# Second layer of a fused attention and feed-forward kernel: products and units of a step in longer runs

## The chip, the cores and the metric
The kernel runs on one NeuronCore of a Trainium2 chip. The metric is the device time of one execution in microseconds. Three executions of the kernel before took 962.70, 963.16 and 963.23 us; the median is 963.16 us. Two such times that lie within 0.2% of each other cannot be told apart.

## The reference
Attention with an exponential feature map, then two feed-forward layers over 2304 tokens, with model width 512 and inner width 2048. The change touches the last line alone.

```python
x = attn_out.transpose(0, 2, 1, 3).reshape(B * S, H * D)      # 2304 x 512
h = x @ w_in                                                  # first layer
x = (h * cos(h)) @ w_out
h = x @ moe2_w_in                                             # second layer
r = maximum(h, 0.0)
out = (r * r) @ moe2_w_out
```

## The kernel before
Every float32 operand of a matmul is split into a high and a low part that PE can multiply fast; each product of two matrices is three matmuls (high-high, high-low, low-high) that add into one PSUM bank.

The second layer goes in 24 **steps** s = 0 to 23: three groups of 768 tokens (NG = 3), and in each group eight pairs of 128-row chunks of the inner width (NP = 8, pair p = s % 8). In each step the first matrix product, of 2 x 2 blocks, is done with seven block products in place of eight (a Strassen-like scheme, PRODUCTS): `product(s, k)`, k = 0 to 6, is six matmuls of 384 columns (L611). The products write two PSUM banks in turn (`banks`): an even k writes bank a, an odd k bank b, and the banks swap at each step. `quarters(s, k)` stands behind each product and takes the results out: ScalarE copies s1 (L628), s2 (L637) and s3 (L642) from bank a after k = 0, 2 and 4; VectorE adds b to s1 and s2 (L634, L640) and subtracts it from s3 (L647); after k = 6 VectorE adds a (L652), and ScalarE takes a's positive part (L655) and squares it (L656). So the four quarters "11", "12", "21", "22" of the activation arise. `square` (L625) squares the positive part; `hi_lo` (L592 on ScalarE, L593 on VectorE) splits a quarter into its high and low part. Since k = 2, 4 and 6 add to or overwrite bank a, each has to wait for the copy of two products earlier.

The second matrix product of step s is done one step later, as twelve **units** of three matmuls of 512 columns each (`unit(s - 1, n)`, L666). Units 0 to 5 use the quarters "11" and "21", units 6 to 11 "12" and "22". At the end of a group the units' six sums are evicted (L676 on ScalarE, L678 on VectorE) and stored.

All engines run their instructions in the order in which they are written out; so where a line of Python stands decides what stands in front of what in each engine's queue. `second_layer` goes through the steps 1 to 24 (24 has units alone) and in each through k = 0 to 6: a product, its quarters, then two units (`UNITS_AT = (2, 2, 2, 2, 2, 1, 1)`), `refill` and `read_back`. `read_back` issues the loads of step s + 2's weights on SP's queue, once a product has used the old ones. `refill` makes the combinations of x for the next group in steps 7, 8, 15 and 16 (roundings on ScalarE, L451; differences and remainders on VectorE, L445 and L452). Step 0's products stand among the last matmuls of the first layer (L385, 512 columns).

Until step 6 `convert_late` also converts the sixteen tiles of the layer's second weight matrix, which arrive as 64-bit words. Each tile has a table of times (`LATE_AT`, in steps of 1/7): load on SP; 2 later two word operations on ScalarE (L238, L240); 2 later three operations on VectorE (L259, L261, L268) and an add on GpSimd (L263); 2 later the rounding on ScalarE (L281) and the remainder on VectorE (L285). What is due is written out after each k.

Of the kernel before, what the change touches and what calls it, by code (L numbers as in the profile page):

```python
# [12 lines left out]
ACTF = mybir.ActivationFunctionType  # L13
# [13 lines left out]
    ("A11", "B11", 0, True), ("A12", "B21", 1, True), ("S2", "T2", 0, False), ("S4", "B22", 1, True),  # L27
    ("S3", "T3", 0, False), ("A22", "T4", 1, True), ("S1", "T1", 0, False),
)
UNITS_AT = (2, 2, 2, 2, 2, 1, 1)  # L30
AHEAD_TILES = tuple(("in", n) for n in range(16))
AHEAD_FIRST, AHEAD_NEXT, AHEAD_STAGE, AHEAD_LOAD = 14.0, 8.6, 7.0, 9.5
LATE_AT = (-1, 1, 3, *range(5, 44, 3))
# [130 lines left out]
def attention_ffn_kernel(  # L164
# [11 lines left out]
    nc = tc.nc  # L176
# [12 lines left out]
    def f(t):  # L189
        return t.bitcast(F32)  # L190

    with tc.manual_schedule():
# [11 lines left out]
        def work(tag, shape, dtype=F32, name=None):  # L204

            return shared.tile(shape, dtype, tag=tag, name=name or tag, bufs=BUFS[tag])

        def bank(tag, shape=(P, 512), name=None):
            return ps.tile(list(shape), F32, tag=tag, name=name or tag, bufs=BUFS[tag])
# [225 lines left out]
        NG, NP = NT // GROUP, KFF // 2  # L435
        raw_x, wc, spill, h2_t, g2_t, b2 = {}, {}, {}, {}, {}, {}
# [17 lines left out]
        def x_parts(name):  # L454
            if name == "B11":
                return b2["B11"]
            return [b2["xc"][:, i, XCOMBOS.index(name)] for i in range(2)]
# [17 lines left out]
        def w_piece(s, i, hl):  # L475
            if i == 3:
                return wc["half"][:, s % 2, hl]
            return wc[s, i][:, hl]
# [98 lines left out]
        def convert_late(now):  # L577
            while late_events and late_events[0][0] < now + 1:
                late_events.pop(0)[1]()

        def quarter(s, name):
            if s % 2 == 0:
                tag = {"11": "e", "21": "e", "12": "kq1", "22": "kq1"}[name]
                g = work(tag, [P, 2, HALF], F32R, "g")
            else:
                g = w_slot({"11": 28, "21": 29, "12": 30, "22": 31}[name], F32R, [P, 2, HALF], "g")
            g2_t[s, name] = g
            return g

        def hi_lo(s, name):  # L590
            g, t = quarter(s, name), h2_t.pop((s, name))
            nc.scalar.activation(out=g[:, 0], in_=t, func=ACTF.Copy)  # L592
            nc.vector.tensor_tensor(out=g[:, 1], in0=t, in1=f(g[:, 0]), op=ALU.subtract)  # L593

        def banks(s):
            return [b2["m"][(s + i) % 2][:, 0:HALF] for i in range(2)]

        def product(s, k):
            if k == 0 and s == 0:
                b2["m"] = [bank("pj", name="m") for _ in range(2)]  # L600
            p = s % NP
            wn, xn, to, start = PRODUCTS[k]
            i = next(i for i in range(4) if wn in PIECES[i])
            o = 2 * P * PIECES[i].index(wn)
            wh, wl = (w_piece(s, i, hl)[:, o:o + 2 * P] for hl in range(2))
            xh, xl = x_parts(xn)
            m = banks(s)[to]
            for q in range(2):
                sl = slice(q * P, (q + 1) * P)
                for n, (l, r) in enumerate(((wh, xh), (wh, xl), (wl, xh))):  # L610
                    nc.tensor.matmul(  # L611
                        out=m, lhsT=l[:, sl], rhs=r[:, q], start=start and q == 0 and n == 0, stop=q == 1 and n == 2,
                        skip_group_check=True,
                    )

        def quarters(s, k):

            a, b = banks(s)

            def new(name, tag="pq"):  # L620
                t = h2_t[s, name] = work(tag, [P, HALF], F32, "t")
                return t

            def square(t):
                nc.vector.scalar_tensor_tensor(out=t, in0=t, scalar=0.0, in1=t, op0=ALU.max, op1=ALU.mult)  # L625

            if k == 0:
                nc.scalar.activation(out=new("s1", "kq"), in_=a, func=ACTF.Copy)  # L628
                if s > 0:
                    hi_lo(s - 1, "12")  # L630
                    hi_lo(s - 1, "22")
            elif k == 1:
                t = new("11")
                nc.vector.tensor_tensor(out=t, in0=b, in1=h2_t.pop((s, "s1")), op=ALU.add)  # L634
                square(t)
            elif k == 2:
                nc.scalar.activation(out=new("s2", "kq"), in_=a, func=ACTF.Copy)  # L637
                hi_lo(s, "11")
            elif k == 3:
                nc.vector.tensor_tensor(out=new("12"), in0=b, in1=h2_t.pop((s, "s2")), op=ALU.add)  # L640
            elif k == 4:
                nc.scalar.activation(out=new("s3", "pk"), in_=a, func=ACTF.Copy)  # L642
                t = h2_t[s, "12"]
                nc.vector.tensor_tensor(out=t, in0=t, in1=h2_t[s, "s3"], op=ALU.subtract)
            elif k == 5:
                t = new("21")
                nc.vector.tensor_tensor(out=t, in0=h2_t.pop((s, "s3")), in1=b, op=ALU.subtract)  # L647
                square(t)
            else:
                hi_lo(s, "21")  # L650
                t = h2_t[s, "12"]
                nc.vector.tensor_tensor(out=t, in0=a, in1=t, op=ALU.add)  # L652
                square(t)
                t = new("22")
                nc.scalar.activation(out=t, in_=a, func=ACTF.Relu)  # L655
                nc.scalar.activation(out=t, in_=t, func=ACTF.Square)  # L656

        def unit(s, n):
            m, f_ = divmod(n, 2)
            if s == 0 and n == 0:  # L660
                acc[:] = [bank(tag, name="acc") for tag in ("pj", "pj", "kv", "nm", "nm", "tp")]
            p = s % NP
            g, w = g2_t[s, f"{f_ + 1}{m // 3 + 1}"], weights[1, 1, 2 * p + f_]
            sl = slice(m % 3 * P, (m % 3 + 1) * P)
            for i, (l, r) in enumerate(((0, 0), (1, 0), (0, 1))):
                nc.tensor.matmul(  # L666
                    out=acc[m], lhsT=g[:, l, sl], rhs=w[:, r], start=p == 0 and f_ == 0 and i == 0,
                    stop=p == NP - 1 and f_ == 1 and i == 2,
                )
            if p == NP - 1 and f_ == 1:  # L670
                if m >= 3 and s == NG * NP - 1:
                    dst = work("pq", [P, DM], F32, "ot")
                else:
                    dst = mag_p.tile([P, DM], F32, tag="mag", name="ot")
                if m % 2:
                    nc.scalar.activation(out=dst, in_=acc[m], func=ACTF.Copy)  # L676
                else:
                    nc.vector.tensor_copy(dst, acc[m])  # L678
                o = s // NP * GROUP + m * P
                nc.sync.dma_start(out=out[o:o + P, :], in_=dst)  # L680

        def refill(s, k):
            g, p = divmod(s, NP)
            if p == NP - 2 and k == 6 and g + 1 < NG:
                for name in "XYZW":
                    x_load(g + 1, name)
            todo = ()
            if p == NP - 1 and g + 1 < NG:
                todo = ((), (0,), (3, 4), (1,), (2, 5), (6,), ())[k]
            elif p == 0 and g > 0:  # L690
                todo = {0: (7,), 1: (8,), 2: (9,), 3: (10,)}.get(k, ())
            for i in todo:
                fill_steps[i]()

        def read_back(s, k):
            if s + 2 < NG * NP:
                i = {1: 0, 3: 1, 5: 3, 6: 2}.get(k)
                if i is not None:
                    read_piece(s + 2, i)

        def second_step(s, k):
            if s < NG * NP:
                product(s, k)
                quarters(s, k)
            elif k == 0:
                for name in ("12", "22"):
                    hi_lo(s - 1, name)
            if s > 0:
                n0 = sum(UNITS_AT[:k])
                for n in range(n0, n0 + UNITS_AT[k]):  # L710
                    unit(s - 1, n)
            refill(s, k)
            read_back(s, k)

        def second_layer():
            for s in range(1, NG * NP + 1):
                for k in range(7):
                    second_step(s, k)
                    convert_late(7 * s + k)

        def share(j, i):
            if j == 0 and i >= START_0:
# [29 lines left out]
        def feed_forward(between):  # L752
            for j in range(len(BLOCKS)):
# [26 lines left out]
                if j + 1 == LAST_0:  # L780
                    while ahead_events:
                        ahead_events.pop(0)[1]()
                    b2["xc"] = const.tile([P, 2, len(XCOMBOS), 2, HALF], F32R, tag="xbuf", name="xc")
            second_layer()


# [3 lines left out]
        with ExitStack() as actx:  # L790
# [172 lines left out]
            run, steps = {}, {}  # L963
# [164 lines left out]
```

## Time and profile before
| | |
|---|---|
| median of three runs | 963.16 us |
| the profiled execution's own time | 963.75 us |
| its span | 962.0 us |
| PE busy | 953.5 us |
| VectorE busy | 657.4 us |
| ScalarE busy | 536.9 us |
| GpSimd busy | 169.0 us |
| mean granted clock of PE | 0.999 |

The profiled execution is 0.6 us longer than the median, and its span leaves out 1.75 us at its two ends. A busy PE is not a PE at its peak: matmuls overlap, so a matmul is listed at 0.33 to 0.40 us while the next starts 0.17 to 0.24 us after it. What a matmul costs is read from the distance of the starts.

### The profile page before, as it was taken

To read this page: it belongs to the slowest core of one execution; us is meant where nothing else is said; L and a number is where in the kernel's file an instruction comes from. 1 tells how busy PE (TensorE), PEld (TensorE's weight loads), DVE (VectorE), ACT (ScalarE), POOL (GpSimd) and SP (SyncE) were. 2 spreads that over 40 slices of the span, in tenths; PEclk is the share of its full clock that TensorE was granted. 3 is DMA by queue.
4 is the path that set the end of the run, shared out by engine and by line. 5 is a ranking of instruction groups with operands and counts; after the bars stand their busy time and mean duration, and the time that the engine had idled before them with its cause. 6 is when DMAs were issued, how large, how long until landed. Compare 5 with 4: busy or idle time off the path is not lost.

```text
span 962.0 us, 15555 instructions
## 1 busy us (share of the span) xinstructions
PE 953.5 (99%) x5865; PEld 824.9 (86%) x5865; DVE 657.4 (68%) x1137; ACT 536.9 (56%) x1053; POOL 169.0 (18%) x146
## 2 busy tenths in 40 slices
PE   8999999999999999999999999999999999999998
PEld 7878888788899888888888888989889898989897
DVE  6787887589967777867867667777663444744344
ACT  4988886667766656666655654555352323423223
POOL 1666765100002033213200011221000000000000
PEclk9999999999999999999999999999999999999999
DMA  7566633152021155334335206656563435544411
GB/s 245 174 204 229 189 121 101 32 204 79 1 89 41 29 190 168 120 131 155 132 132 149 71 22 208 199 184 190 172 194 112 121 113 184 164 138 126 118 36 65
DMA packets 52282, 128.26 MB, mean 133 GB/s; under 512 B 6384, under 2 KB 12144, under 8 KB 52208
## 3 DMA queue, kind: packets, MB, share of 16 engines
q1 hardware_dynamic: 52064, 127.21, 41.2%
q8 instruction: 46, 0.75, 0.3%
q14 instruction: 28, 0.23, 0.1%
q10 hardware_dynamic: 144, 0.07, 0.0%
HBM read 102.99 MB, written 24.19 MB: 132 GB/s over the span
## 4 chain that ended last, share of the span: by engine, by line
PE 94%; DMA 2%; ACT 2%; DVE 1%; POOL 0%; SPq 0%; issue 0%; DVEq 0%; ACTq 0%; POOLq 0%
PE acc L385 21%; PE acc L666 20%; PE m L611 18%; PE h L314 7%; PE h L315 7%; PE h L316 7%; PE kv L867 5%; PE nm L913 3%; PE pj L833 2%; PE nm L921 2%; PE tp L890 1%; PE kv L875 1%; PE pj L842 1%; DMA raw<-in_dram 1%; ACT eq L901 1%; ACT e L859 0%
## 5 line engine op out<-in xcount | busy, mean ns | idle before, releaser
L666 PE MATMUL acc<-w,g 128*128 128x512 f32 x864 | 226.0, 394 | 0.0
L385 PE MATMUL acc<-g,w 128*128 128x512 f32 (+1 forms) x960 | 208.6, 368 | 0.0
L385 PEld LDWEIGHTS acc<-g,w 128*128 128x128 f32 x960 | 168.0, 189 | 30.5 <-DVE g L345 0.6
L666 PEld LDWEIGHTS acc<-w,g 128*128 128x128 f32 x864 | 159.7, 188 | 23.3
L611 PE MATMUL m<-xc,wc 128*128 128x384 f32 x864 | 173.7, 336 | 0.8 <-DVE t L634 0.8
L611 PEld LDWEIGHTS m<-xc,wc 128*128 128x128 f32 x864 | 154.5, 188 | 14.2 <-DVE t L634 1.3
L314 PE MATMUL h<-xs,w 128*128 128x512 f32 (+1 forms) x320 | 117.9, 369 | 0.0
L315 PE MATMUL h<-xs,w 128*128 128x512 f32 (+1 forms) x320 | 117.7, 368 | 0.0
L316 PE MATMUL h<-xs,w 128*128 128x512 f32 (+1 forms) x320 | 117.7, 368 | 0.0
L593 DVE TENSOR_TENSOR g<-t,g 128x384 fp32r<-128x384 f32 x96 | 53.6, 579 | 77.5 <-ACT g L592 77.4
L342 ACT ACTIVATE g<-tr 128x512 fp32r<-128x512 f32 (+1 forms) x80 | 47.0, 589 | 69.2 <-PE acc L385 46.7
L263 POOL TENSOR_TENSOR mag<-mag,raw 128x512 int32<-128x512 int32 x36 | 48.1, 1337 | 213.1 <-ACT tr L335 92.1
L592 ACT ACTIVATE g<-t 128x384 fp32r<-128x384 f32 x96 | 47.3, 518 | 64.8 <-DVE t L625 64.5
L337 DVE SCALAR_TENSOR_TENSOR tr<-tr,h 128x512 f32<-128x512 f32 (+1 forms) x80 | 50.5, 631 | 35.5 <-ACT tr L335 35.2
L345 DVE TENSOR_TENSOR g<-tr,g 128x512 fp32r<-128x512 f32 (+1 forms) x80 | 52.8, 660 | 24.7 <-ACT g L342 24.7
L314 PEld LDWEIGHTS h<-xs,w 128*128 128x128 f32 x320 | 60.3, 189 | 10.2 <-issue 0.2
L316 PEld LDWEIGHTS h<-xs,w 128*128 128x128 f32 x320 | 60.3, 188 | 10.1
L315 PEld LDWEIGHTS h<-xs,w 128*128 128x128 f32 x320 | 60.4, 189 | 9.9
L848 DVE TENSOR_REDUCE m<-pj 128x4 f32<-128x512 f32 (+1 forms) x80 | 49.9, 624 | 19.3 <-PE pj L833 11.7
L867 PEld LDWEIGHTS kv<-v,e 128*128 128x128 f32 x512 | 60.1, 192 | 3.4 <-issue 1.8
L867 PE MATMUL kv<-v,e 128*128 128x65 f32 x512 | 62.1, 274 | 0.7 <-ACT e L859 0.6
L330 DVE SCALAR_TENSOR_TENSOR tr<-tr,h 128x512 f32<-128x512 int32 (+1 forms) x80 | 50.2, 628 | 16.0 <-ACT tr L328 15.5
(92 smaller groups left out, 1339.8 us busy)
## 6 DMA issues: line engine op xcount, KB each, us to landing
wc<-sp SPq DMA_DIRECT2D x72, 512.0 KB
raw<-in_dram SPq DMA_DIRECT2D x48, 512.0 KB
xbuf<-in_dram SPq DMA_DIRECT2D x16, 512.0 KB
sp<-xbuf SPq DMA_DIRECT2D x15, 512.0 KB
kq<-in_dram SPq DMA_DIRECT2D x16, 384.0 KB
wc<-sp SPq DMA_DIRECT2D x24, 256.0 KB
v<-in_dram SPq DMA_DIRECT2D x16, 330.0 KB
dn<-db SPq DMA_DIRECT2D x32, 144.0 KB
```

What stands on the lines that cost most here:

```text
L314: nc.tensor.matmul(out=hps, lhsT=ih[:, kk, :], rhs=xh, start=kk == 0, stop=False)
L315: nc.tensor.matmul(out=hps, lhsT=ih[:, kk, :], rhs=xl, start=False, stop=False)
L316: nc.tensor.matmul(out=hps, lhsT=il[:, kk, :], rhs=xh, start=False, stop=kk == KDM - 1)
L330: nc.vector.scalar_tensor_tensor(out=r, in0=t.bitcast(I32), scalar=-C1, in1=h_t[c], op0=ALU.mult, op1=ALU.add)
L337: nc.vector.scalar_tensor_tensor(out=t, in0=r, scalar=1.0, in1=h_t.pop(c), op0=ALU.subtract, op1=ALU.mult, reverse0=True)
L345: nc.vector.tensor_tensor(out=g[:, 1], in0=t, in1=f(g[:, 0]), op=ALU.subtract)
L385: nc.tensor.matmul(out=acc[m][:, 0:n], lhsT=l, rhs=r, start=c == 0 and i == 0, stop=c == KFF - 1 and i == 2)
L593: nc.vector.tensor_tensor(out=g[:, 1], in0=t, in1=f(g[:, 0]), op=ALU.subtract)
L611: nc.tensor.matmul(out=m, lhsT=l[:, sl], rhs=r[:, q], start=start and q == 0 and n == 0, stop=q == 1 and n == 2, skip_group_check=True,)
L666: nc.tensor.matmul(out=acc[m], lhsT=g[:, l, sl], rhs=w[:, r], start=p == 0 and f_ == 0 and i == 0, stop=p == NP - 1 and f_ == 1 and i == 2,)
L848: nc.vector.tensor_reduce(out=m[:, 0:n], in_=pj[:, 0:n, :], axis=AX.X, op=ALU.max, apply_absolute_value=True)
L867: nc.tensor.matmul(out=acc[:, s, h, 0:D + 1], lhsT=e[:, t, s, :], rhs=v_t[u][:, t, h, 0:D + 1], start=t == 0 and h == 0 and s == 0, stop=F ...
```

## The change
The second layer's steps are written out in runs. `SHORT_RUNS` does products 0 and 1, four units, products 2 and 3, four units, products 4, 5 and 6, four units. `LONG_RUNS` does all seven products and then all twelve units. A step is long from step 7 on (`LONG_FROM`) if its pair is neither the first nor the last of its group; else it is short.

The quarters' later work moves with it. The square of "11" stands one product later, its `hi_lo` too. After the last product six pieces of work (square and `hi_lo` of "21", square of "12", square of "22", `hi_lo` of "12" and of "22") are put on a list, `owed`, of which one is written out behind each of the next units; a long step first writes out what is still owed. `convert_late` is called after each unit, with a time that goes on by 7/12, and no longer after each product.

```diff
--- before.py
+++ after.py
@@ -27,7 +27,9 @@
     ("A11", "B11", 0, True), ("A12", "B21", 1, True), ("S2", "T2", 0, False), ("S4", "B22", 1, True),
     ("S3", "T3", 0, False), ("A22", "T4", 1, True), ("S1", "T1", 0, False),
 )
-UNITS_AT = (2, 2, 2, 2, 2, 1, 1)
+SHORT_RUNS = (((0, 1), 4), ((2, 3), 4), ((4, 5, 6), 4))
+LONG_RUNS = (((0, 1, 2, 3, 4, 5, 6), 12),)
+LONG_FROM = 7
 AHEAD_TILES = tuple(("in", n) for n in range(16))
 AHEAD_FIRST, AHEAD_NEXT, AHEAD_STAGE, AHEAD_LOAD = 14.0, 8.6, 7.0, 9.5
 LATE_AT = (-1, 1, 3, *range(5, 44, 3))
@@ -613,6 +615,8 @@
                         skip_group_check=True,
                     )
 
+        owed = []
+
         def quarters(s, k):
 
             a, b = banks(s)
@@ -626,18 +630,15 @@
 
             if k == 0:
                 nc.scalar.activation(out=new("s1", "kq"), in_=a, func=ACTF.Copy)
-                if s > 0:
-                    hi_lo(s - 1, "12")
-                    hi_lo(s - 1, "22")
             elif k == 1:
                 t = new("11")
                 nc.vector.tensor_tensor(out=t, in0=b, in1=h2_t.pop((s, "s1")), op=ALU.add)
-                square(t)
             elif k == 2:
                 nc.scalar.activation(out=new("s2", "kq"), in_=a, func=ACTF.Copy)
-                hi_lo(s, "11")
+                square(h2_t[s, "11"])
             elif k == 3:
                 nc.vector.tensor_tensor(out=new("12"), in0=b, in1=h2_t.pop((s, "s2")), op=ALU.add)
+                hi_lo(s, "11")
             elif k == 4:
                 nc.scalar.activation(out=new("s3", "pk"), in_=a, func=ACTF.Copy)
                 t = h2_t[s, "12"]
@@ -645,15 +646,16 @@
             elif k == 5:
                 t = new("21")
                 nc.vector.tensor_tensor(out=t, in0=h2_t.pop((s, "s3")), in1=b, op=ALU.subtract)
-                square(t)
             else:
-                hi_lo(s, "21")
                 t = h2_t[s, "12"]
                 nc.vector.tensor_tensor(out=t, in0=a, in1=t, op=ALU.add)
-                square(t)
                 t = new("22")
                 nc.scalar.activation(out=t, in_=a, func=ACTF.Relu)
-                nc.scalar.activation(out=t, in_=t, func=ACTF.Square)
+                owed.extend((
+                    lambda: square(h2_t[s, "21"]), lambda: hi_lo(s, "21"), lambda: square(h2_t[s, "12"]),
+                    lambda: nc.scalar.activation(out=t, in_=t, func=ACTF.Square),
+                    lambda: hi_lo(s, "12"), lambda: hi_lo(s, "22"),
+                ))
 
         def unit(s, n):
             m, f_ = divmod(n, 2)
@@ -699,24 +701,31 @@
                     read_piece(s + 2, i)
 
         def second_step(s, k):
-            if s < NG * NP:
-                product(s, k)
-                quarters(s, k)
-            elif k == 0:
-                for name in ("12", "22"):
-                    hi_lo(s - 1, name)
-            if s > 0:
-                n0 = sum(UNITS_AT[:k])
-                for n in range(n0, n0 + UNITS_AT[k]):
-                    unit(s - 1, n)
+            product(s, k)
+            quarters(s, k)
             refill(s, k)
             read_back(s, k)
 
         def second_layer():
-            for s in range(1, NG * NP + 1):
-                for k in range(7):
-                    second_step(s, k)
-                    convert_late(7 * s + k)
+            steps = NG * NP
+            for _ in range(2):
+                owed.pop(0)()
+            for s in range(1, steps + 1):
+                n, now = 0, 7.0 * s
+                runs = LONG_RUNS if s >= LONG_FROM and 0 < s % NP < NP - 1 else SHORT_RUNS
+                while runs is LONG_RUNS and owed:
+                    owed.pop(0)()
+                for ks, units in runs:
+                    if s < steps:
+                        for k in ks:
+                            second_step(s, k)
+                    for _ in range(units):
+                        unit(s - 1, n)
+                        n += 1
+                        if owed:
+                            owed.pop(0)()
+                        convert_late(now)
+                        now += 7 / 12
 
         def share(j, i):
             if j == 0 and i >= START_0:
```

Three places of the built program show it. First PE in step 9: before, where the pattern of six and six goes on, with runs of three units' matmuls at the end of the step; and now, where it is a long step (behind the last runs of the short step 8).

```order
L611 MATMUL m<-xb,wc 128x384 x6
L666 MATMUL acc<-w,g 128x512 x6
L611 MATMUL m<-xc,wc 128x384 x6
L666 MATMUL acc<-w,g 128x512 x6
L611 MATMUL m<-xc,wc 128x384 x6
L666 MATMUL acc<-w,g 128x512 x6
```

```order
L613 MATMUL m<-xc,wc 128x384 x18
L668 MATMUL acc<-w,g 128x512 x12
L613 MATMUL m<-xb,wc 128x384 x6
L613 MATMUL m<-xc,wc 128x384 x36
L668 MATMUL acc<-w,g 128x512 x36
```

The 36 unit matmuls that stood in seven runs now stand in one, and so do the 42 product matmuls (the product with xb and six with xc).

Second, ScalarE in step 1, from the copy s2 (of bank m_5999) on; mag and raw are buffers of the weight conversion, w its rounded result, t a quarter or copy, g its high part. Before:

```order
L637 ACTIVATE t_6182<-m_5999 128x384
L592 ACTIVATE g_6184<-t_6162 128x384
L281 ACTIVATE w_6193<-mag_6059 128x512
L642 ACTIVATE t_6224<-m_5999 128x384
L238 ACTIVATE mag_6233<-raw_6196 128x512
L240 ACTIVATE raw_6196<-raw_6196 128x512
L281 ACTIVATE w_6249<-mag_6173 128x512
```

And with the change, to the copy s3:

```order
L637 ACTIVATE t_6186<-m_5999 128x384
L594 ACTIVATE g_6197<-t_6135 128x384
L240 ACTIVATE mag_6215<-raw_6172 128x512
L242 ACTIVATE raw_6172<-raw_6172 128x512
L283 ACTIVATE w_6221<-mag_6160 128x512
L643 ACTIVATE t_6232<-m_5999 128x384
```

The copy s3 (L642, now L643) stood directly behind one rounding; the two word operations and the next tile's rounding, which followed it, now stand ahead of it.

Third, ScalarE in step 3, again from s2 to s3. Before:

```order
L637 ACTIVATE t_6473<-m_5999 128x384
L592 ACTIVATE g_6475<-t_6452 128x384
L238 ACTIVATE mag_6484<-raw_6444 128x512
L240 ACTIVATE raw_6444<-raw_6444 128x512
L281 ACTIVATE w_6503<-mag_6418 128x512
L642 ACTIVATE t_6514<-m_5999 128x384
```

And with the change:

```order
L637 ACTIVATE t_6475<-m_5999 128x384
L594 ACTIVATE g_6486<-t_6440 128x384
L283 ACTIVATE w_6494<-mag_6410 128x512
L240 ACTIVATE mag_6512<-raw_6497 128x512
L242 ACTIVATE raw_6497<-raw_6497 128x512
L643 ACTIVATE t_6521<-m_5999 128x384
```

The rounding has moved ahead of the two word operations, which now stand directly in front of s3; they belong to another tile than before (the one that is loaded later).

## Rows read from the trace of the kernel before

**Rows 1.** The page: busy time by engine; shares of the chain that ended last.
```profile
PE 953.5 (99%) x5865; PEld 824.9 (86%) x5865; DVE 657.4 (68%) x1137; ACT 536.9 (56%) x1053; POOL 169.0 (18%) x146
...
PE 94%; DMA 2%; ACT 2%; DVE 1%; POOL 0%; SPq 0%; issue 0%; DVEq 0%; ACTq 0%; POOLq 0%
```

**Rows 2.** Timeline of PE, ordinary step: start, duration, line, shape, count.
```profile
729.97 1.22 PE L611 MATMUL m<-xb,wc 128*128 128x384 f32 x6
731.03 1.55 PE L666 MATMUL acc<-w,g 128*128 128x512 f32 x6
...
745.66 1.22 PE L611 MATMUL m<-xb,wc 128*128 128x384 f32 x6
```

**Rows 3.** Timeline of PE: runs around step 0, step 1, and the last step.
```profile
576.69 2.92 PE L385 MATMUL acc<-g,w 128*128 128x512 f32 x12
579.45 3.31 PE L611 MATMUL m<-xc,wc 128*128 128x384 f32 x18
582.60 2.92 PE L385 MATMUL acc<-g,w 128*128 128x512 f32 x12
585.36 2.27 PE L611 MATMUL m<-xc,wc 128*128 128x384 f32 x12
587.47 1.20 PE L611 MATMUL m<-xb,wc 128*128 128x384 f32 x6
...
604.48 1.22 PE L611 MATMUL m<-xb,wc 128*128 128x384 f32 x6
...
948.88 9.04 PE L666 MATMUL acc<-w,g 128*128 128x512 f32 x39
```

**Rows 4.** Who waited for whom, PE, 570 to 958 us: total, times, longest.
```profile
PE m L611 <- DVE t L634: 0.8, 1, 0.8
```

**Rows 5.** Timeline of VectorE, steps 2 and 3.
```profile
604.62 0.55 DVE L652 TENSOR_TENSOR t<-m,t 128x384 f32<-128x384 f32 x1
605.20 0.56 DVE L625 SCALAR_TENSOR_TENSOR t<-t 128x384 f32<-128x384 f32 x1
605.68 0.42 DVE L259 TENSOR_SCALAR mag<-mag 128x512 f32<-128x512 f32 x1
...
606.59 0.69 DVE L268 SCALAR_TENSOR_TENSOR mag<-raw,mag 128x512 int32<-128x512 int32 x1
...
625.52 0.69 DVE L285 TENSOR_TENSOR w<-mag,w 128x512 fp32r<-128x512 f32 x1
```

**Rows 6.** Timeline of ScalarE, steps 2 to 4.
```profile
613.30 0.68 ACT L238 ACTIVATE mag<-raw 128x512 f32<-128x512 f32 x1 [1.79 <-DMA raw<-in_dram]
613.88 0.65 ACT L240 ACTIVATE raw<-raw 128x512 int32<-128x512 uint32 x1
615.47 0.49 ACT L642 ACTIVATE t<-m 128x384 f32<-128x384 f32 x1 [0.93 <-PE m L611]
615.86 0.62 ACT L281 ACTIVATE w<-mag 128x512 fp32r<-128x512 f32 x1
...
634.03 0.67 ACT L238 ACTIVATE mag<-raw 128x512 f32<-128x512 f32 x1 [2.39 <-DMA raw<-in_dram]
```

**Rows 7.** Timeline of GpSimd, step 1.
```profile
601.44 1.40 POOL L263 TENSOR_TENSOR mag<-mag,raw 128x512 int32<-128x512 int32 x1 [4.44 <-ACT raw L240]
```

**Rows 8.** Timeline of SP's queue: one weight load of 512 KB, issued.
```profile
608.58 0.38 SPq L472 DMA_DIRECT2D raw<-in_dram  x1
```

**Rows 9.** Groups of instructions by line: busy us, mean ns | idle before.
```profile
L452 DVE TENSOR_TENSOR xc<-xr,xc 128x768 fp32r<-128x768 f32 x21 | 20.0, 953 | 3.0 <-ACT xc L451 2.6
...
L451 ACT ACTIVATE xc<-xr 128x768 fp32r<-128x768 f32 x21 | 17.6, 836 | 4.4 <-DVE xr L445 4.4
```

**Rows 10.** Busy time by engine in the last 2 us; PEclk is the granted clock.
```profile
960.00:962.00 2.00, 0.00 (x0) 0.00 (x0) 0.00 (x0) 0.00 (x0) 0.00 (x0) 0.54 0.21 77
```

**Rows 11.** Timeline of PE at the program's start.
```profile
1.58 2.50 PE L820 MATMUL nm<-eq 128*128 128x512 f32 x5 [1.58 <-DVE eq L814]
...
8.24 1.18 PE L820 MATMUL nm<-eq 128*128 128x512 f32 x4
```

## The prediction

> **What bounds the kernel now.** I read the page first: PE is busy for 99% of the span and carries 94% of the chain that ended last [rows 1]. So only two things can move the time: how long PE's instructions stand apart, and how long PE waits. Next comes PE's timeline in the second layer. Ordinary steps are equal to 0.01 us: a step (42 product matmuls of 384 columns, 36 unit matmuls of 512) takes 745.66 - 729.97 = 15.69 us, and six products take 731.03 - 729.97 = 1.06 us [rows 2]. One step is longer: step 1 takes 604.48 - 587.47 = 17.01 us [rows 3], so 1.3 us go to waits there. The list of who waited shows 0.8 us of that as one wait of a product for L634 on VectorE, and no other row for PE in the whole second layer [rows 4]. All else is spacing.
>
> **Spacing: what longer runs give.** The old program holds runs of the new lengths, around step 0, where products stand among the first layer's 512-column matmuls [rows 3]. Twelve 512-column matmuls between products take 579.45 - 576.69 = 2.76 us, 18 products 582.60 - 579.45 = 3.15 us, and 12 products 587.47 - 585.36 = 2.11 us. So six more in a running run cost 3.15 - 2.11 = 1.04 us. For long runs of units the last step shows 39 in 9.04 us, 0.39 of it the last one's own length, so 38 spacings in 8.65 us [rows 3]; 36 of them are 8.20.
> A step of the form 2, 2, 3 products with 4, 4, 4 units is then 3 x 2.76 + 2 x 2.11 + 3.15 = 15.65 us. A step of seven products and twelve units is 3.15 + 24 x 1.04 / 6 + 8.20 = 15.51 us. Against 15.69 that is 0.04 and 0.18 us. The order of the built program has 11 steps of the first form (1 to 8, 15, 16, 23) and 12 of the second (9 to 14, 17 to 22); step 24 is units alone and stays. **Gain: 11 x 0.04 + 12 x 0.18 = 2.6 us.**
> The Trainium skill (TensorE: Matmul & The Clock Gate, section "Back-to-back issue gap") has a gap that depends on the columns alone, N/2.4 + 2.5 ns; by it a step lasts the same in any order and this gain is nil. The rows disagree: the same six products cost 1.04 or 1.06 us by what stands ahead of them.
>
> **Inside the run of seven.** A product may write its bank only when the copy of two products earlier is out of it, so each read has one product, 1.04 us, to finish. The matmul's result is 0.16 us behind its slot (2.27 listed, 2.11 taken [rows 3]); a ScalarE read takes 0.49 us [rows 6], a VectorE read 0.55 us [rows 5]; with 0.05 us for each hand-over (an estimate: 605.20 - 604.62 is 0.03 more than the 0.55 listed [rows 5]) it is 0.75 and 0.81 us. It fits, and the 18 products in a row above passed one such turn without a wait. Cost 0.
>
> **The old wait.** The wait in step 1 is for the sum L634, which stood in VectorE's queue behind deferred copies and weight conversion. In the new order that sum is recorded right after its product, ahead of these. The 1.3 us go, but what is late next is the copy of the fifth product (s3, new L643), which the seventh product needs.
>
> **New waits: weight conversion ahead of s3.** Until step 6 the second weight matrix is converted: load, two ScalarE word operations, three VectorE operations, a GpSimd add, a ScalarE rounding (L281, new L283), a VectorE remainder. Before, these were spread over the step; between the fifth and the seventh product stood three units and one product. Now nothing is recorded during the products, all of it during the units, and between the fifth and the seventh product stands one product. Whatever ScalarE holds when the run 5, 6, 7 begins delays PE almost in full.
> Durations, as spacing to the next one where one follows: a VectorE operation of 384 columns 0.48, or 0.58 if the next reads it; the three conversions 0.91 for two and 0.69 to the third's end, 1.65 with the hand-over; 0.6 for a 512-column operation listed at 0.69, with the same overlap [rows 5]. ScalarE: 384 columns 0.49, or 0.39 to the next, words 0.58, rounding 0.62 [rows 6]. GpSimd's add 1.40 [rows 7], 1.45 with the hand-over.
> *Step 1.* The order shows ScalarE: s2, copy, two words, rounding, s3. One chain runs from the end of step 0's last product (587.47 + 0.16 + 0.05 = 587.7): its sum 0.47; two evictions 1.2; square 0.58, copy on ScalarE 0.55, remainder 0.5; sum, square, weight remainder 0.48 + 0.48 + 0.60; three conversions of the next tile 1.65; add 1.45; rounding 0.62; then VectorE: remainder 0.60, remainder 0.47, square 0.48, sum 0.55, remainder 0.47; conversions 1.65; add 1.45; rounding 0.55; s3 0.54. Sum 15.3, so s3 is done at 603.0. PE without waits begins the seventh product at 587.47 + 2.11 + 2.76 + 2.11 + 2.76 + 2.10 = 599.3. **Wait 3.7 us**, of which some half a microsecond falls at earlier instructions. Bounds: 2.7 (hand-overs and add cheaper) to 4.3 (a late weight load in front).
> *Step 3.* Here two words stand directly ahead of s3, and their load is issued only after the read-back that waits for product 4: 0.6 us after that product. Load to first word took 613.30 - 608.58 = 4.72 us [rows 6, 8]. With two words 1.16 and s3 0.54 it ends at 7.0; PE is there after four units and two products, 4.86. **Wait 2.1 us**, bounds 1.2 to 3.
> *Step 4.* Chain from product 4: 0.2 + 0.47 + 0.55 + 1.65 + 1.45 + 0.55 + 0.54 = 5.4 against 4.86: **0.4 us** after rounding down for overlap; 0 to 0.8. In steps 2, 5 and 6 the add was recorded a whole run earlier: nothing.
> *Steps 8 and 16.* In the step ahead, VectorE and ScalarE refill the x combinations [rows 9]. Between its fifth product and the next step's second one now stand drain and hand-over 0.2, s3 0.49, rounding 0.84, remainder 0.95, difference 0.95, rounding 0.84, remainder 0.95, sum 0.55 and relu 0.49, with hand-overs about 6.3; PE's way is 2.10 + 2.76 + 1.06 = 5.9. *Steps 9 and 17.* An output eviction (as long as a word operation), a square, two copies and s1 now end 0.2 + 0.58 + 3 x 0.41 + 0.49 = 2.5 us after the first product starts; the third needs the bank after 2.1. **Each 0.4 us, four times 1.5 us**; bounds 0 to 2.4.
> Queues: the read-backs on SP only move earlier within a step, with almost two steps until their use; GpSimd's adds are the ones counted. Cost 0; without that slack a 512 KB load would cost up to 4.7 us.
>
> **Sum.** -2.6 - 1.3 + 3.7 + 2.1 + 0.4 + 1.5 = +3.8 us, taken as **+3.6**, since the chains count every hand-over in full. The profiled execution took 963.75 us (span 962.0), so 967.4 on its scale. It lies 0.6 us above the median of the runs, 963.16, which I forecast from: **966.8 us**. A measurement can tell about 0.2%, 1.9 us, from no change.
>
> **Rivals.**
> 1. *Faster.* Conversion keeps ahead: ScalarE has rounded its tile before product 5 ends in steps 1 and 3, because loads and adds start earlier than I chain them. For it: ScalarE is only 56% busy. Against: ScalarE's queue already stood 2.39 us for a load [rows 6], and PE was spared only by the distance. It decides if the tile's add is done 0.6 us before product 5 ends. Then -2.6 - 1.3 + 1.5: 960.8. Chance 0.06.
> 2. *No change.* One chain is shorter, say step 1's waits are 1.4 and the small ones vanish in part: 963.9. Chance 0.19.
> 3. *The clock falls* in the wait of step 1. In this trace PE's one wait in the layer is 0.8 us [rows 4]. After its last work, at 948.88 + 9.04 = 957.9 [rows 3], the granted clock reads 0.54 in the slice from 960 [rows 10]. So some 3 us of waiting may be enough. At the program's start five 512-column matmuls take 2.50 us, at 8.24 four take 1.18 [rows 11]: 1.2 against 2.4 GHz, with 2 to 6.7 us between. Half of that is 1 to 3.3 us: 969.0. Chance 0.15. The Trainium skill (same page, Part 1) says an idle PE is throttled to half rate; the last slice agrees.
> 4. *Switches cost nothing*, and the 0.25 us by which a step exceeds its steady spacing comes from elsewhere: the 2.6 us stay, 969.4. The runs of [rows 3] speak against it. Chance 0.03.
>
> **How the numbers follow.** My forecast has 0.57, with 965.1 to 968.8 from the bounds of its waits. Slower: 0.57 + 0.15 + 0.03 = 0.75; same 0.19; faster 0.06. The range 964.0 to 969.2 leaves out the faster case, the lower part of the second rival and the tail of the third, 0.17 or so.
>
> **What would show it.** Long steps of 15.5 us and short ones of 15.65; a PE wait of about 3 us for L643 in step 1, one near 2 us in step 3, ScalarE idle there behind a GpSimd add and a weight load. I am wrong if step 1 takes under 18 us or step 3 under 16.5, or if the long steps show waits between products.

## The result and the profile after

The changed kernel takes **969.38 us** (median of six executions, 968.30 to 972.84); the kernel before took 963.04 us beside it (six, 962.12 to 963.30). The ratio is 1.0072, with the interval 1.0056 to 1.0088. That is slower, as forecast, but by 6.3 us and not by 3.6, and 0.2 us beyond the upper end of the range.

The page of the profiled execution (972.84 us, the longest of the six; span 971.0 us) answers [rows 1] with this:

```profile
PE 957.3 (99%) x5865; PEld 827.3 (85%) x5865; DVE 645.4 (66%) x1133; ACT 533.5 (55%) x1050; POOL 169.1 (17%) x146
...
PE 93%; ACT 2%; DMA 2%; DVE 2%; issue 0%; POOL 0%; SPq 0%; ACTq 0%; POOLq 0%; DVEq 0%
```

PE still bounds the kernel, for 9 us longer, of which it is busy for 3.8. The rest are waits that [rows 4] did not have. The list of PE's waits from 570 us on (total, times, longest):

```profile
PE m L613 <- ACT t L643: 5.3, 3, 2.9
PE m L613 <- ACT t L653: 0.6, 2, 0.3
PE m L613 <- ACT t L632: 0.4, 2, 0.2
```

The wait for L634 is gone, and the copy s3 (L643) is what is late next, three times. PE's timeline shows where. In step 1, and in the first product of step 2:

```profile
587.50 1.20 PE L613 MATMUL m<-xb,wc 128*128 128x384 f32 x6
588.83 1.31 PE L613 MATMUL m<-xc,wc 128*128 128x384 f32 x6
589.98 3.30 PE L668 MATMUL acc<-w,g 128*128 128x512 f32 x12
593.12 2.27 PE L613 MATMUL m<-xc,wc 128*128 128x384 f32 x12
595.23 3.56 PE L668 MATMUL acc<-w,g 128*128 128x512 f32 x12
...
603.75 1.32 PE L613 MATMUL m<-xc,wc 128*128 128x384 f32 x6 [2.87 <-ACT t L643]
604.91 4.51 PE L668 MATMUL acc<-w,g 128*128 128x512 f32 x12
609.26 1.22 PE L613 MATMUL m<-xb,wc 128*128 128x384 f32 x6
```

Step 1 lasts 609.26 - 587.50 = 21.76 us. Step 3 (19.49 us) and step 4 (16.33) in the same view:

```profile
638.91 2.06 PE L613 MATMUL m<-xc,wc 128*128 128x384 f32 x6 [2.01 <-ACT t L643]
640.76 3.79 PE L668 MATMUL acc<-w,g 128*128 128x512 f32 x12
644.38 1.23 PE L613 MATMUL m<-xb,wc 128*128 128x384 f32 x6
...
646.49 2.92 PE L668 MATMUL acc<-w,g 128*128 128x512 f32 x12
649.25 2.27 PE L613 MATMUL m<-xc,wc 128*128 128x384 f32 x12
...
656.80 1.32 PE L613 MATMUL m<-xc,wc 128*128 128x384 f32 x6 [0.41 <-ACT t L643]
657.96 2.92 PE L668 MATMUL acc<-w,g 128*128 128x512 f32 x12
```

Twelve units that take 649.25 - 646.49 = 2.76 us elsewhere took 609.26 - 604.91 = 4.35 us behind step 1's wait. Behind step 3's they took 3.62 us, and the six products ahead of them 640.76 - 638.91 = 1.85 us, where 656.80 to 657.96 shows 1.16 behind a wait without this. Busy time of PE in stretches (length, busy time with the number of matmuls, granted clock, DMA share, GB/s) says why:

```profile
604.80:608.20 3.40, 3.40 (x11) 0.54 0.52 154
639.00:642.40 3.40, 3.40 (x10) 0.53 0.23 36
```

**The clock fell** to 1.2 GHz (0.54 and 0.53 as means of these stretches), twice, right after the two long waits. It cost (4.35 - 2.76) + (3.62 - 2.76) + (1.85 - 1.16) = 3.1 us. From the start of step 1 to the last matmul the kernel before took 370.07 us and this execution 379.42: 9.35 us, 6.2 of them without the clock. The medians differ by 6.3 us, and four of the six executions have a granted clock of 1.000 (968.30, 968.88, 969.28, 969.47 us), the other two 0.998 and 0.996. So the typical loss is waits, and the clock stands on top of it in some executions. Not every wait is in the list above: of the 4.4 us by which step 1's seventh product came late (603.75 against 587.50 + 11.8), 1.3 us had gone before, in pieces too short for it (the second product 0.27 us late, the two runs of units ahead of the long wait 3.14 and 3.40 us in place of 2.76).

A long step, in PE's timeline (the 36 units, then the next step's 42 products):

```profile
731.68 8.36 PE L668 MATMUL acc<-w,g 128*128 128x512 f32 x36
739.88 1.23 PE L613 MATMUL m<-xb,wc 128*128 128x384 f32 x6
740.95 6.43 PE L613 MATMUL m<-xc,wc 128*128 128x384 f32 x36
747.22 1.08 PE L668 MATMUL acc<-w,g 128*128 128x512 f32 x4
```

It takes 8.20 + 7.34 = 15.54 us (others up to 15.57); short ones without a wait take 15.64. Against 15.69 [rows 2] the spacing gain is there.

### The profile page after: what moved, and what is told of

It is laid out like the page before. It is cut to its first block, busy times and chain, and to the rows that moved or that the text cites. A ratio compares the mean times of both kernels' runs of the same rounds, so it can differ in the third digit from the quotient of the medians.

```text
span 971.0 us, 15613 instructions
## 1 busy us (share of the span) xinstructions
PE 957.3 (99%) x5865; PEld 827.3 (85%) x5865; DVE 645.4 (66%) x1133; ACT 533.5 (55%) x1050; POOL 169.1 (17%) x146
## 4 chain that ended last, share of the span: by engine, by line
PE 93%; ACT 2%; DMA 2%; DVE 2%; issue 0%; POOL 0%; SPq 0%; ACTq 0%; POOLq 0%; DVEq 0%
PE acc L387 20%; PE acc L668 19%; PE m L613 17%; PE h L316 7%; PE h L318 7%; PE h L317 7%; PE kv L876 5%; PE nm L922 3%; PE pj L842 3%; DMA raw<-in_dram 2%; PE nm L930 2%; PE tp L899 1%; PE kv L884 1%; PE pj L851 1%; DVE xc L454 0%; ACT e L868 0%
## 5 line engine op out<-in xcount | busy, mean ns | idle before, releaser
L668 PE MATMUL acc<-w,g 128*128 128x512 f32 x864 | 208.2, 395 | 0.2
L668 PEld LDWEIGHTS acc<-w,g 128*128 128x128 f32 x864 | 163.2, 190 | 33.9 <-DVE g L595 1.4
L613 PE MATMUL m<-xc,wc 128*128 128x384 f32 x864 | 161.1, 338 | 6.5 <-ACT t L643 5.3
L613 PEld LDWEIGHTS m<-xc,wc 128*128 128x128 f32 x864 | 152.3, 188 | 10.9 <-ACT t L643 6.3
L595 DVE TENSOR_TENSOR g<-t,g 128x384 fp32r<-128x384 f32 x96 | 51.5, 554 | 25.4 <-ACT g L594 25.3
L635 DVE TENSOR_TENSOR t<-m,t 128x384 f32<-128x384 f32 x24 | 13.3, 556 | 80.9 <-PE m L613 80.9
```

The costliest lines, as they stand in the source:

```text
L613: nc.tensor.matmul(out=m, lhsT=l[:, sl], rhs=r[:, q], start=start and q == 0 and n == 0, stop=q == 1 and n == 2, skip_group_check=True,)
L668: nc.tensor.matmul(out=acc[m], lhsT=g[:, l, sl], rhs=w[:, r], start=p == 0 and f_ == 0 and i == 0, stop=p == NP - 1 and f_ == 1 and i == 2,)
```

## The experiments

My theory: weight conversion on ScalarE, now bunched behind the products, stands ahead of s3, and only one product lies between s3's own product and the one that needs its bank; in step 1 a chain through the GpSimd add holds it, in step 3 a late weight load. A rival: the lost time is the clock, or sits in the long runs. All eight start from the changed kernel; ratios are to the kernel before, run beside them (963.13 us in 15 executions for runs 1 to 4, 963.17 in 33 for runs 5 to 8). A step is counted from its first product to the next step's; the start of step 1 itself lies at 585.8 to 588.2 us in these traces, for reasons ahead of the change, so steps tell more than single spans.

**1. No conversion behind the units 4 to 7** (ahead of the run 5, 6, 7).

```diff
-                        convert_late(now)
+                        if not 4 <= n - 1 < 8:
+                            convert_late(now)
```

> Weight conversion is written out behind units 0 to 3 and 8 to 11 of a step only, so none of the middle four units' conversion stands on ScalarE ahead of s3. Theory (conversion in ScalarE's queue ahead of s3 holds the seventh product): the waits for s3 in steps 1, 3 and 4 (3.0, 2.2 and 0.6 us) shrink to under 0.3 us in sum and the granted clock stays 1.00; some of it comes back as waits of units, since the conversion now bunches, up to 2 us; 963 to 966 us. Rival (one product between the fifth and the seventh is too little for the read itself): the waits stay where they are, 968 to 970 us.

Measured: 970.52 us (five executions, 968.85 to 972.57), ratio 1.0075 (1.0062 to 1.0087). PE's largest waits (what is left out comes to 1.2 us, none of it for s3):

```profile
PE m L613 <- ACT t L632: 2.7, 4, 1.2
PE acc L668 <- ACT g L594: 2.3, 1, 2.3
```

Not one wait for s3 is left, with one product between its own and the seventh as in the changed kernel; so conversion was what delayed it. But the time did not come back: packed tighter, the conversion delays s1 (L632) four times, and once the high part for a unit (L594) for 2.3 us, behind two words whose load was late; there the clock fell again. The theory names the culprit rightly; I was wrong that there is room for it elsewhere in a step of three runs.

**2. Loads two sevenths of a step earlier**, from the fourth late tile on.

```diff
-                events += stages(("out", n), LATE_AT[n], LATE_STAGE, LATE_STAGE, load, split)
+                events += stages(("out", n), LATE_AT[n], LATE_STAGE, LATE_STAGE + 2 * (n >= 3), load, split)
```

> The loads of the second weight matrix from tile 3 on are issued 4 instead of 2 time units ahead of the word operations. Theory: step 3's wait (2.2 us) is the load that lands late and goes, with the clock fall behind it; step 1's wait (3.0 us) is the chain over the GpSimd add and stays at 2.3 us or more; 966 to 968 us. Rival (all three waits have one cause, the crowded ScalarE queue): step 3's wait stays over 1.5 us, 968.5 us or more.

Measured: 966.90 us (five, 966.65 to 968.89), 1.0039 (1.0026 to 1.0053). Step 3 is 15.64 us, its wait gone; step 4 keeps its 16.33 and step 1 has 21.41, with 2.85 us of waiting and the clock fall behind it (a granted clock of 0.997 or 0.998 in all five executions). Step 3's wait was the load alone. In the changed kernel ScalarE's timeline shows that load, issued by SP at 632.79:

```profile
637.28 0.66 ACT L240 ACTIVATE mag<-raw 128x512 f32<-128x512 f32 x1 [4.70 <-DMA raw<-in_dram]
637.84 0.64 ACT L242 ACTIVATE raw<-raw 128x512 int32<-128x512 uint32 x1
638.38 0.47 ACT L643 ACTIVATE t<-m 128x384 f32<-128x384 f32 x1
```

**3. The late tiles' add on VectorE**, not on GpSimd.

```diff
-            return nc.gpsimd if layer == 1 or n < NEARLY - 1 else nc.vector
+            return nc.gpsimd if (n[0] == "in" if layer == 1 else n < NEARLY - 1) else nc.vector
```

> The adds of the second weight matrix's conversion go from GpSimd (1.3 us, and 0.2 us until it starts) to VectorE (0.7 us). Theory: two adds lie on step 1's chain, one on step 4's; step 1's wait for s3 falls from 3.0 to 1 to 2 us, step 4's from 0.6 to nothing, step 3's stays near 2; 966.5 to 968.5 us. Rival (the late load alone sets step 1's wait): step 1 stays within 0.4 us of 3.0.

Measured: 968.13 us (five, 967.13 to 968.56), 1.0050 (1.0037 to 1.0063). Step 4 is 15.64 us, its wait gone; step 1 waits 2.06 us for s3 where it was 2.87 and takes 19.63 us; step 3 keeps 19.52. PE's timeline has the products behind the waits of step 1 and of step 3:

```profile
601.91 1.32 PE L613 MATMUL m<-xc,wc 128*128 128x384 f32 x6 [2.06 <-ACT t L643]
...
635.56 2.29 PE L613 MATMUL m<-xc,wc 128*128 128x384 f32 x6 [2.08 <-ACT t L643]
```

So step 4 and a part of step 1 are the GpSimd chain. The two waits are equally long, yet only the second was followed by a slow stretch (2.29 us listed for six products, against 1.32; the granted clock of the 3.4 us from each on is 0.51, against 1.00).

**4. Short steps in four runs**: products 1-2, 3-4, 5-6, 7 with three units behind each, so that three units stand between s3's product and the seventh. Since conversion is written out behind units, the edit moves it too: six units and not eight now stand ahead of s3, and what was due behind the seventh and the eighth comes after it.

```diff
-SHORT_RUNS = (((0, 1), 4), ((2, 3), 4), ((4, 5, 6), 4))
+SHORT_RUNS = (((0, 1), 3), ((2, 3), 3), ((4, 5), 3), ((6,), 3))
```

> Short steps become products 0 1, three units, 2 3, three units, 4 5, three units, 6, three units; everything else as changed. Between the fifth and the seventh product stand three units and one product, 3.1 us in place of 1.04. Theory: the waits for s3 go in all steps, clock 1.00 throughout; short steps lose their 0.05 us gain; the waits at steps 9 and 17 stay or grow to 0.9 us each; 961.5 to 964 us. Rival (the conversion is late for PE whatever stands between): waits of 2 us or more remain in steps 1 to 4, 966 us or more.

Measured: 963.56 us (eleven, 962.63 to 964.47), 1.0004 (0.9995 to 1.0013). PE's waits:

```profile
PE m L613 <- ACT t L632: 1.4, 2, 0.7
PE m L613 <- ACT t L637: 0.8, 1, 0.8
```

No conversion was taken away, and none of the waits for s3 is left; step 3 takes 15.71 us and step 1 17.75. The clock was 1.000 in this trace. But the distance is not what did it. ScalarE's timeline in step 1, then the seventh product in PE's:

```profile
598.15 0.47 ACT L643 ACTIVATE t<-m 128x384 f32<-128x384 f32 x1
...
602.10 0.63 ACT L283 ACTIVATE w<-mag 128x512 fp32r<-128x512 f32 x1 [1.79 <-POOL mag L265]
```

```profile
601.05 1.23 PE L613 MATMUL m<-xc,wc 128*128 128x384 f32 x6
```

The rounding that stood directly ahead of s3 in the changed kernel now stands behind it, and so do step 1's two words ahead of that rounding; in step 3 it is the two words (631.59, behind s3 at 629.54). In steps 1 to 6 s3 begins 0.03 to 0.33 us after its product has ended and is done 2.4 us or more ahead of the seventh product. Had the rounding at 602.10 stayed in front, s3 would have ended near 603.1 (an estimate, with the 0.54 and 0.47 us that the rounding and s3 take in the changed kernel), 2 us too late in spite of the distance. So what the run shows is the order in ScalarE's queue, as run 1 does; distance by itself was not tried. The wait for s1 in steps 9 and 17, each the first long step behind a short one, has grown from 0.2 to 0.7 us.

**5. As 4, and long steps begin one pair later** in a group.

```diff
-                runs = LONG_RUNS if s >= LONG_FROM and 0 < s % NP < NP - 1 else SHORT_RUNS
+                runs = LONG_RUNS if s >= LONG_FROM and 1 < s % NP < NP - 1 else SHORT_RUNS
```

> As the kernel with four runs, and the second step of a group is short too, so 10 long steps in place of 12. Theory: the wait of 0.9 us at steps 9 and 17 stands there because an output eviction, a square and two copies are ahead of s1 with two products to go; with three units in between it goes. Two long steps less cost 2 x 0.17 us. 963.5 - 1.7 + 0.3 = 962.1 us, 961.3 to 962.9. Rival (the wait moves on to steps 10 and 18): no change, 963.3 to 963.9.

Measured: 963.11 us (eleven, 961.98 to 965.63), 1.0001 (0.9992 to 1.0010). The waits in steps 9 and 17 are gone (15.71 us); one of 0.9 us in step 1 stays. By the steps this should be some 1.1 us under run 4; the medians show 0.45, and their intervals overlap, so this gain is seen in the trace and not in the times.

**6. Runs 5, 2 and 3 together.** The edits are those above.

> As e5, with the weight loads 4 units ahead and the conversion's add on VectorE. Theory: only step 1's remaining wait (0.9 us) is touched; 961 to 962.5 us, clock 1.00. Rival (with three units between, conversion is off PE's path altogether): the same as e5 within 0.3 us.

Measured: **961.59 us** (eleven, 961.07 to 962.47), 0.9986 (0.9978 to 0.9995), under both kernels (0.16% under the kernel before, less than two medians of three could tell apart, but with these 11 and 33 executions the interval leaves out 1). From 570 us on PE has no row of waits at all. Step 1 goes from 587.34 to 603.78, 16.44 us in place of run 5's 17.91, which is nearly all of the 1.52 us between the medians. Eight of the ten long steps take 15.52 to 15.55; all other ordinary steps take 15.71 to 15.73, the two long ones that follow a short one among them (there the third product comes 0.2 us late, behind s1, in pieces too short for the list).

**7. As 4, with no long steps.**

```diff
-LONG_FROM = 7
+LONG_FROM = 99
```

> As the kernel with four runs, but no long step. Theory: a long step gives 0.16 us against a step of four runs, and the two waits at steps 9 and 17 take 1.7; without both 963.5 - 1.7 + 12 x 0.16 = 963.7 us, and every step from 2 on is 15.7 us. Rival (long runs give nothing): 962 us or less.

Measured: 964.12 us (eleven, 963.04 to 967.48), 1.0014 (1.0006 to 1.0023). Each step from 2 on takes 15.71 us: 21 x 0.02 = 0.4 us more than before, and step 1's 17.48 makes another 0.5. So the long steps are no loss: in the traces the steps from 2 to 22 take 1.3 us more than in run 5, which has ten long ones. The medians differ by 1.0 us, with intervals that just overlap.

**8. The changed kernel's runs with the edits of 2 and 3.**

> The changed kernel with its own runs, weight loads 4 units ahead and the add on VectorE. Theory: step 3's and step 4's waits go, step 1's falls to 1.3 to 2 us, and the clock stays at 1.00; step 1 is 18 to 19 us long, steps 2 to 7 15.64; 964.5 to 966 us. Rival (the two mends work on the same wait): step 1 stays as with the add alone (19.6 us with its clock fall), 966 us or more.

Measured: 964.31 us (eleven, 963.24 to 965.97), 1.0012 (1.0003 to 1.0021). Step 1 takes 18.17 us, with one wait of 1.5 us for s3; steps 2 to 7 take 15.64, steps 8 and 16 still 16.25, 9 and 17 16.01. The clock did not fall behind the 1.5 us. The two mends take away different waits: step 3 belongs to the load, step 4 to the add, and step 1 to both (with 1.6 us taken off where the clock fell, it loses 4.5 us over 15.64 in the changed kernel, 4.2 in run 2, 4.0 in run 3, 2.5 here: each mend alone leaves the other to hold the chain). Its steps give, against before, +1.16 in step 1, +1.11 in 8 and 16, +0.65 in 9 and 17, and -1.65 in the others: +1.3 us, and the medians differ by 1.14.

## Why the prediction was right in kind and short in size

**The mechanism** is what the prediction named: the longer runs gain little, the old wait goes, and s3 is late behind weight conversion, in the steps named. Runs 1 and 4, where conversion no longer stands ahead of s3, show it, and runs 2, 3 and 8 show what held it. Rivals 1 and 2 (conversion keeps ahead, or one chain is shorter) are out, as the seventh product came later than forecast in steps 1, 3 and 4 (by 4.4, 2.2 and 0.6 us, against 3.7, 2.1 and 0.4); so is rival 4 (switches cost nothing), as long steps are shorter than before. One argument against rival 1 was misread: the words that stood 2.39 us for their load in the kernel before did not spare PE by distance. They stood behind step 3's s3, in ScalarE's timeline:

```profile
631.16 0.49 ACT L642 ACTIVATE t<-m 128x384 f32<-128x384 f32 x1
```

**The step that failed is the sum of waits and gains**, above all its term for step 1: a wait priced at 3.7 us, with bounds of 2.7 to 4.3, made the seventh product 4.4 us late (1.3 us of it ahead of the long wait, where I had half a microsecond). All other terms but that of the other short steps came out a little worse than forecast too, and I had rounded the sum down.

| term | forecast | measured, clock taken off |
|---|---|---|
| step 1: new wait less old wait and spacing | +2.4 | 21.76 - 1.59 - 17.01 = +3.2 |
| step 3 | +2.1 | 19.49 - 1.55 - 15.69 = +2.25 |
| step 4 | +0.4 | +0.65 |
| steps 8 and 16 | +0.7 | 2 x 0.55 = +1.1 |
| steps 9 and 17 | +0.4 | 2 x 0.33 = +0.65 |
| the other ten long steps | -1.8 | -1.3 |
| the other short steps, the last | -0.2 | -0.3 |
| sum, before rounding | +3.8, taken as +3.6 | +6.2 |

*Step 1* was sized too small by 0.8 us. I chained s3's end to 603.0; the product behind it began at 603.75. The chain holds up to the first conversion (592.56 worked out, 592.58 in the trace) and then breaks at the first rounding, worked out for 595.66. ScalarE's timeline:

```profile
594.65 0.67 ACT L240 ACTIVATE mag<-raw 128x512 f32<-128x512 f32 x1 [2.81 <-DMA raw<-in_dram]
595.23 0.66 ACT L242 ACTIVATE raw<-raw 128x512 int32<-128x512 uint32 x1
595.78 0.51 ACT L594 ACTIVATE g<-t 128x384 fp32r<-128x384 f32 x1
596.20 0.62 ACT L283 ACTIVATE w<-mag 128x512 fp32r<-128x512 f32 x1
...
602.69 0.63 ACT L283 ACTIVATE w<-mag 128x512 fp32r<-128x512 f32 x1 [1.65 <-POOL mag L265]
603.23 0.47 ACT L643 ACTIVATE t<-m 128x384 f32<-128x384 f32 x1
```

The load for the two words at its head, in the timeline of SP's queue:

```profile
588.10 0.38 SPq L474 DMA_DIRECT2D raw<-in_dram  x1
588.88 2.48 SPq L407 DMA_DIRECT2D x<-ot  x4
```

It was first used 594.65 - 588.10 = 6.55 us after its issue, not after the 4.72 of [rows 6, 8] (four stores of the first layer are issued right behind it; whether they slow it was not tried). So the words came late, a high part (L594) and the rounding queued behind them, and the rounding began at 596.20: 0.54 us. In run 2, where the load is issued earlier, this rounding begins 8.35 us into the step and not 8.70; so 0.35 us of it is the load. That is the "late weight load in front" that I had only in the bounds. The trace of the kernel before could have told me: its load of step 1, issued at 588.07, has its first use at 594.22, 6.15 us later. ScalarE's timeline there:

```profile
594.22 0.68 ACT L238 ACTIVATE mag<-raw 128x512 f32<-128x512 f32 x1 [0.99 <-DMA raw<-in_dram]
```

The rest is small; a part of it is the hand-over to GpSimd, which the chain passes twice. First VectorE's timeline, then GpSimd's:

```profile
600.46 0.69 DVE L270 SCALAR_TENSOR_TENSOR mag<-raw,mag 128x512 int32<-128x512 int32 x1
```

```profile
601.38 1.28 POOL L265 TENSOR_TENSOR mag<-mag,raw 128x512 int32<-128x512 int32 x1 [5.66 <-DMA raw<-in_dram]
```

GpSimd begins at 601.38, 0.23 us after VectorE's end at 600.46 + 0.69, where I took 0.05 (in the kernel before it was 0.23 too); the add itself, 1.28 and not 1.40, gave most of that back.

*The waits of 0.4 us* in steps 8, 9, 16 and 17 were priced as the wait alone. PE's timeline in step 8:

```profile
707.64 1.22 PE L613 MATMUL m<-xb,wc 128*128 128x384 f32 x6
709.19 1.31 PE L613 MATMUL m<-xc,wc 128*128 128x384 f32 x6 [0.33 <-ACT t L653]
710.34 2.92 PE L668 MATMUL acc<-w,g 128*128 128x512 f32 x12
```

The second product begins 1.55 us after the first, where 1.07 is usual: 0.48. And the six matmuls behind the wait take 710.34 - 709.19 = 1.15 us in place of 1.04: a wait costs another 0.1 us of spacing. The same 0.1 is in steps 1 and 4, where no fall of the clock hides it (603.75 to 604.91 and 656.80 to 657.96).

*"Inside the run of seven ... Cost 0"* was wrong by about 0.05 us for each of the long steps. The 36 units took the 8.20 us forecast; the 42 products took 7.34 to 7.37 and not 7.31. No wait is listed within the runs of these ten steps, so the read of a bank fits; but once in a run a start slips by some 5 ns, and the spacing behind it begins anew (below). In the long step above it is the start of the fourth product, 0.2 us after VectorE's read of its bank has ended; that the read caused it is likely and not shown.

*Rival 3* put one fall of the clock, at 2.2 us, on top of the forecast: 969.0. That number nearly met the median by chance: four of the six executions kept the full clock, and the waits alone make up the loss. As a mechanism it is real: behind waits of 2.0 to 2.9 us the clock fell in the changed kernel and in runs 1, 2 and 3, and never in a trace whose longest wait was 1.5 us or less. A fall cost some 1.6 us, and the profiled execution had two. The Trainium skill (TensorE: Matmul & The Clock Gate, Part 1) has an idle PE throttled to half rate; these rows agree on the level (0.53 and 0.54), but the clock stayed up behind one wait of 2.06 us (run 3). The gap in that page's section "Back-to-back issue gap", which it gives for a matmul by itself, goes by the columns alone; the steps of 15.69, 15.64 and 15.54 us with the same matmuls show that here the order counts as well.

## What to carry to other kernels

Before bunching one engine's work to make another engine's runs longer, count for each buffer in the run how much work lies between its reader and its next writer, and what then stands ahead of the reader in its own queue. Run 4 undid all the large waits without taking any conversion away, because the late pieces of it came to stand behind the reader. A chain of many hand-overs can come out longer than the sum of its parts, as step 1's did, since one late load holds all behind it: do not round such a sum down. Price a wait with what follows it, the spacing that starts anew and the chance that the clock falls, on top of the forecast.

## What the runs showed that I had not expected

**What a switch costs is spread over some nine matmuls.** Distances of the starts, in ns, from the single matmuls of the traces (run 7, then products of a long step of the changed kernel):

```
products behind units   171 175 177 185 176 182 173 173 174 173 173 174
units behind products   229 233 236 224 231 236 228 233 231
42 products, 17th on    173 179 175 174 171 175 177 185 176 182 173 173
```

Steady spacing is 173.3 and 226.7 ns, so 42 products and 36 units would take 7.28 + 8.16 = 15.44 us. The first six products behind a switch take 26 ns more than that and the first nine units 41: 0.07 us for a pair. One pair gives 15.51, three 15.64, four 15.71, as measured (long steps with up to 0.06 more, for slips within the run). Before, runs of six units and six products ended ahead of the rest of the pattern, and a step with seven pairs took 15.69. So four runs of nine units are slower than the old order, though they switch less often; that is run 7.

**The clock does not fall behind every long wait.** Waits of 2.06 and 2.08 us in one execution of run 3 ended differently. Run 2 had a clock of 0.997 or 0.998 in all five executions, the changed kernel one under 1.000 in two of six, with the same wait in step 1 as far as the traces go (2.85 and 2.87 us). What decides it stays open, as only one execution of each kernel has a trace. The longest executions of runs 5 and 7 (965.63 and 967.48 us) read 0.998 too; what they waited for is not known.

**A wait that was left.** In run 8 step 1 still waits 1.5 us and steps 8, 9, 16 and 17 some 0.5 us each with the changed kernel's runs; I did not try to mend these without the fourth run.
